# Order of the VectorE's copies, a second PSUM bank for the first projection, and the slots of the queries' transposes in a fused attention and MLP kernel

## The chip, the core and the metric

The kernel runs on one core of a Trainium2 chip. The metric is the device time of one launch in microseconds. Five engines run their own instruction streams and meet through semaphores: PE (TensorE, with its weight loads shown as PEld), DVE (VectorE), ACT (ScalarE), POOL (GpSimd) and SP (SyncE, which here only issues transfers). Matmul results go to PSUM, which this kernel holds as one tile `ps` of eight banks of 512 float32 columns and divides by hand.

## The reference

For each of 8 x 8 heads of 576 tokens and 64 dimensions: scores, a threshold at the row's maximum less `tau`, softmax over what is left, and the product with the values. The 4608 rows of 512 go through an MLP with a hard swish.

```python
def _attn_ref(q, k, v, tau):
    scores = scale * np.matmul(q, k.transpose(0, 1, 3, 2))
    thresh = np.max(scores, axis=-1, keepdims=True) - tau
    scores = np.where(scores >= thresh, scores, -1000000000.0)
    scores = scores - np.max(scores, axis=-1, keepdims=True)
    attn = np.exp(scores)
    attn = attn / (np.sum(attn, axis=-1, keepdims=True) + 1e-09)
    return np.matmul(attn, v).astype(np.float32)

def _moe_ref(x, w_in, w_out):          # x: 4608 x 512, w_in: 512 x 2048
    h = x @ w_in
    g = h * np.clip(h + 3.0, 0.0, 6.0) / 6.0
    return (g @ w_out).astype(np.float32)
```

## The kernel before, in words

**Slots.** Four heads make a quad, two a pair; there are 16 quads, and two quads are one batch element. A quad is worked in 9 slots: slots 0 to 3 take 128 queries each of the quad's first pair, 4 to 7 of its second pair, slot 8 the 64 left-over queries of both pairs. `n` counts the slots through the kernel, from 0 to 143; "slot 63" below is `n = 63`. The loop over `n` writes every engine's instructions out in order, and each engine runs them in that order; there is no scheduler behind it. A quad that is odd begins at an odd `n`.

**What a slot holds**, in the order of the loop: the two exponentials of the slot before (`sm_exp`, L309, ACT); the row maxima, which also move the scores from PSUM to SBUF (`sm_max`, L296, DVE, two instructions of 128x576) and the bias of the threshold (L299, POOL); one item of the MLP's first projection (`mm1`, L372, PE, eight matmuls for two blocks of 128 features by 256 tokens), its rectifier (`mm1_relu`: L380 on ACT in even slots, L382 on DVE in odd ones) and the product (`mm1_gate`, L387, DVE), called the gate here; the reciprocals of the slot before (`sm_recip`, L312, DVE); in even slots two quarters of a token tile of the second projection (`mm2_part`, L397, PE) and, after a tile's last quarter, its copy (`mm2_out`, L405, DVE); the masks (`sm_mask`, L304, ACT); the jobs that `plan[n]` names; the scores of coming slots (`scores`, L269, or L275 for slot 8; PE); and the normalization of the slot before (`sm_norm`, L317, POOL), which comes behind this slot's biases on POOL and needs L312.

**Jobs.** `av0`, `av0late` and `av1` multiply a pair's attention by its values (`av_main`, L341 and L344 on PE, then a copy to `xT`, L352, DVE); `avr` does the same for the left-over queries (copy L362). `q0` and `q1` transpose the queries of the next quad's first pair and of this quad's second pair. For the first two batch elements they do it on PE (L217) with a copy on DVE (L224), for the others in one DVE instruction (L226). `k0` and `k1` transpose keys on PE, with a copy on ACT (L207) from slot 22 on; `rest` does both for the left-over rows (L238, L240; copies L246 and L207).

**From slot 22 (`N1`) on** the scores of two slots are written together at the end of each odd slot: those of the odd slot in PSUM columns of banks 0, 1, 3 and 4 ("lower"), those of the even one in banks 1, 2, 4 and 5 ("upper"). Banks 2 and 5 also serve the jobs in turn (`bank()`), so a job of an odd slot must have been copied out before the last score matmuls of that slot are written. The first projection has bank 6 (`HB`), the second bank 7 (`OB`), where a token tile accumulates over two even slots.

**The projections' order.** From slot 22 each batch element has 16 items in `todo1`, one to a slot; 18 slots later the next follow. The eighth and the sixteenth item put eight quarters of the second projection into `todo2`, of which two go in each even slot. So bank 7 is in use from slot 30 to 36 and from 38 to 44, and again 18 slots later.

Of the kernel before, what the change touches and what calls it, by code (L numbers as in the profile page):

```python
# [21 lines left out]
def kernel(  # L22
# [20 lines left out]
    N1 = 22  # L43
    HB = 6
    OB = 7
# [74 lines left out]
    def load_v(b):  # L120
        vm = v_pool.tile([P, H, 4 * D], BF16, tag="vm", name="vm")
        vr = vrs[b % 2]
        vsb[b] = (vm, vr)
        for g in range(2):
            vcasts.append(lambda g=g: nc.gpsimd.dma_start(
                out=vm[:, g * 4:g * 4 + 4, :],
                in_=v[b, g * 4:g * 4 + 4, 0:512, :].rearrange("h (p t) d -> p h (t d)", t=4)))
        for a in range(2):
            vcasts.append(lambda a=a: nc.gpsimd.dma_start(
                out=vr[a * 64:(a + 1) * 64, a, :, :],  # L130
                in_=v[b, :, 512:S, :].rearrange("(hp a) p d -> a p hp d", a=2)[a]))
# [78 lines left out]
    def by_pe(pair):  # L210
        return pair // NPAIR < NB
# [77 lines left out]
    def sm_max(sl):  # L289
        sl.s = s_pool.tile([P, 2, S], F32, tag="s", name="s")  # L290
        sl.m = stat_pool.tile([P, 2], F32, tag="m", name="m")
        sl.bias = stat_pool.tile([P, 2], F32, tag="bias", name="bias")
        sl.rsum = stat_pool.tile([P, 2], F32, tag="rsum", name="rsum")
        sl.rinv = stat_pool.tile([P, 2], F32, tag="rinv", name="rinv")
        for i in range(2):
            nc.vector.tensor_scalar(out=sl.s[:, i, :], in0=score_tile(sl.n, i),  # L296
                                    scalar1=1.0, scalar2=None, op0=Alu.mult, op1=Alu.max,
                                    accum_out=sl.m[:, i:i + 1])
            nc.gpsimd.tensor_scalar(out=sl.bias[:, i:i + 1], in0=sl.m[:, i:i + 1], scalar1=-scale, scalar2=tau,  # L299
                                    op0=Alu.mult, op1=Alu.add)  # L300
# [6 lines left out]
    def sm_exp(sl, i):  # L307
        s = sl.s[:, i, :]
        nc.scalar.activation(out=s, in_=s, func=Act.Exp, accum_out=sl.rsum[:, i:i + 1])  # L309

    def sm_recip(sl):
        nc.vector.reciprocal(out=sl.rinv[:], in_=sl.rsum[:])  # L312
# [15 lines left out]
    def pe_transpose(sl):  # L328
        pb = ps_flat[:, 3072:3072 + S].bitcast(BF16).rearrange("p (c t) -> p c t", t=P)
        pn = sl.pn[:].rearrange("p a b -> p (a b)")  # L330
        for c in range(9):
            nc.tensor.transpose(pb[:, c, :], pn[:, c * P:(c + 1) * P], identb[:])
        return lambda: nc.vector.tensor_copy(out=sl.dst, in_=pb)
# [33 lines left out]
    def mm1(item, hb=HB):  # L367
        src, ni, c0, _ = item
        hps = ps[:, hb, :].rearrange("p (n w) -> p n w", n=2)
        for n in range(2):  # L370
            for ki in range(KI):
                nc.tensor.matmul(hps[:, n, :], w_in_sb[:, ki, (ni + n) * P:(ni + n + 1) * P],  # L372
                                 src[:, ki, c0:c0 + 256], start=(ki == 0), stop=(ki == KI - 1))
        return hps


    def mm1_relu(hps, on_act):
        r = r_pool.tile([P, 2, 256], F32, tag="r", name="r")[:]
        if on_act:
            nc.scalar.activation(out=r, in_=hps, func=Act.Relu, bias=three[:])  # L380
        else:
            nc.vector.tensor_scalar(out=r, in0=hps, scalar1=3.0, scalar2=0.0, op0=Alu.add, op1=Alu.max)  # L382
        return r

    def mm1_gate(item, hps, r):
        _, ni, _, g0 = item
        nc.vector.scalar_tensor_tensor(out=gbuf[:, ni:ni + 2, g0:g0 + 256], in0=r, scalar=6.0, in1=hps,  # L387
                                       op0=Alu.min, op1=Alu.mult)
# [24 lines left out]
    todo2 = []  # L413
# [16 lines left out]
    def moe_of_rest(b):  # L430
        items = [((xR[b // 4], ni, 0, M), ()) for ni in range(0, NI, 2)]
        items[-1] = (items[-1][0], [(c, 4, part) for c in (b, b - 2) for part in range(4)])
        return items
# [19 lines left out]
    plan = []  # L453
    for sl in queue:
        quad, slot = sl.quad, sl.slot
        if sl.n < N1:
            jobs = {1 if quad else 2: ["q1"], 2 if quad else 3: ["k1"], 5: ["alloc", "q0"], 6: ["k0"], 7: ["rest"],
                    8: ["av0"]}
            if quad == 0:
                jobs[1] = ["rest0"]  # L460
            else:
                jobs[3], jobs[4] = (["av1"], ["avr"]) if quad == 1 else (["av1", "avr"], [])
        elif quad % 2:
            jobs = {0: ["q1", "av0late"], 1: ["k1"], 4: ["av1", "avr"], 5: ["alloc", "k0"], 6: ["q0"], 7: ["rest"],
                    8: ["av0"]}
        else:
            jobs = {1: ["q1"], 2: ["k1"], 3: ["av1", "avr"], 4: ["alloc", "k0"], 5: ["q0"], 6: ["rest"]}
        if quad + 1 == NQUAD:
            jobs = {s: [j for j in jobs[s] if j not in ("alloc", "k0", "q0", "rest")] for s in jobs}
        plan.append(jobs.get(slot, []))  # L470

    prev = None
    for n, sl in enumerate(queue):
        quad, slot = sl.quad, sl.slot
        b, g = divmod(quad, 2)
        now = n
        if slot in (0, 4):
            pts[2 * quad + slot // 4] = pt_pool.tile([P, 9, 512], BF16, tag="pT", name="pT")
        if slot == 8:
            ptr[quad] = ptr_pool.tile([P, 9, P], BF16, tag="pR", name="pR")  # L480
        if quad == 0 and slot == 0:
            load_quad(1)
        if slot == (4 if quad else 8) and quad + 2 < NQUAD:
            load_quad(quad + 2)
        if slot == 0 and g == 1 and b + 1 < B:
            load_v(b + 1)
        if prev is not None:
            for i in range(2):
                sm_exp(prev, i)
        sm_max(sl)  # L490

        if todo1 or todo3:
            item, then = (todo1 or todo3).pop(0)
            h = mm1(item)
            r = mm1_relu(h, on_act=n % 2 == 0)
            mm1_gate(item, h, r)
            todo2.extend(then)
        copies = pe_transpose(queue[n - 2]) if n > 1 and queue[n - 2].on_chip else None
        if prev is not None:
            sm_recip(prev)  # L500
        if copies:
            copies()
        outs = []


        for _ in range(0 if n % 2 else 2):
            if todo2:
                b2, t2, part = todo2.pop(0)
                mm2_part(b2, t2, part)
                if part == 3:  # L510
                    outs += mm2_out(b2, t2, on_act=False)
        for i in range(2):
            sm_mask(sl, i)
        nxt = 2 * quad + 2
        for job in plan[n]:
            if job == "alloc":
                alloc_qk(quad + 1)
            elif job == "q1":
                transpose_q(2 * quad + 1)()
            elif job == "k1":  # L520
                transpose_k(2 * quad + 1)()
            elif job == "q0":
                transpose_q(nxt)()
            elif job == "k0":
                transpose_k(nxt)()
            elif job == "rest":
                transpose_rest(quad + 1)()
            elif job == "rest0":
                transpose_rest(0, of_k=False)()
            elif job == "av1":  # L530
                av_main(2 * quad - 1)
            elif job == "av0":
                av_main(2 * quad)
            elif job == "av0late":
                av_main(2 * quad - 2)
            elif job == "avr":
                av_rest(quad - 1)
                if quad % 2 == 0:
                    todo1.extend(moe_of(quad // 2 - 1))
                if quad % 8 == 0:  # L540
                    todo3.extend(moe_of_rest(quad // 2 - 1))
        if n == 0:
            warm_up(8)
        if n + 1 < N1:
            scores(n + 1)
        elif n % 2 and n + 2 < len(queue):
            scores(n + 1, n + 2)
        if n < 8:
            warm_up(6)
        if prev is not None:  # L550
            sm_norm(prev)
        flush()
        late.extend(outs)
        start(loads, 1)
        if n < 4 or n > 12:
            start(vcasts, 1)
        if n > 3:
            start(casts, 1 if n < 24 else 2)
        prev = sl
# [80 lines left out]
```

## Time and profile before

| | |
|---|---|
| median of 6 runs | 581.22 us (580.37 to 583.05) |
| the profiled execution | 581.61 us, of which 579.8 us from its first to its last instruction |
| PE busy | 535.4 us (92%) |
| ACT busy | 473.5 us (82%) |
| DVE busy | 424.3 us (73%) |
| POOL busy | 305.4 us (53%) |
| mean granted TensorE clock | 0.997 |

In the profile's rows a time is from the start of the span. `L372` is line 372 of the kernel before. A row of a timeline gives start, length, engine, line, operation, what is written and read, the count of merged instructions and, in brackets, the engine's idle time just before and what ended it. A merged PE row ends later than its last matmul matters: the start of the next PE row is the better mark. The slots repeat closely: the stretch of 18 slots from slot 36 to 53 takes 128.38 to 191.73 us, that from 54 to 71 191.73 to 255.07 us.

### The profile page before, as it was taken

To read this page: it belongs to the slowest core of one execution; us is meant where nothing else is said; L and a number is where in the kernel's file an instruction comes from. 1 tells how busy PE (TensorE), PEld (TensorE's weight loads), DVE (VectorE), ACT (ScalarE), POOL (GpSimd) and SP (SyncE) were. 2 spreads that over 40 slices of the span, in tenths; PEclk is the share of its full clock that TensorE was granted. 3 is DMA by queue.
4 is the path that set the end of the run, shared out by engine and by line. 5 is a ranking of instruction groups with operands and counts; after the bars stand their busy time and mean duration, and the time that the engine had idled before them with its cause. 6 is when DMAs were issued, how large, how long until landed. Compare 5 with 4: busy or idle time off the path is not lost.

```text
span 579.8 us, 12005 instructions
## 1 busy us (share of the span) xinstructions
PE 535.4 (92%) x3998; PEld 328.1 (57%) x3998; DVE 424.3 (73%) x1060; ACT 473.5 (82%) x1012; POOL 305.4 (53%) x646
## 2 busy tenths in 40 slices
PE   8898787899989998999989998999989998989997
PEld 6654454555555565555555665556555665545853
DVE  3788776687878788787878888788868888741731
ACT  4898987898988898999989898888889898851730
POOL 2789867755565555655565556555565455530000
PEclk9999998999999999999999999999999999999999
DMA  5999989986797779997897789995997744552012
GB/s 118 136 137 161 195 131 193 179 155 135 144 164 143 133 154 153 144 166 117 163 160 151 131 137 162 128 162 113 160 152 144 143 101 98 84 116 72 3 36 73
DMA packets 286350, 77.54 MB, mean 134 GB/s; under 512 B 269264, under 2 KB 281808, under 8 KB 286288
## 3 DMA queue, kind: packets, MB, share of 16 engines
q1 hardware_dynamic: 267680, 67.47, 64.2%
q0 software_dynamic: 17408, 8.92, 13.4%
q8 instruction: 31, 0.51, 0.4%
q10 hardware_dynamic: 1200, 0.39, 0.3%
q14 instruction: 31, 0.25, 0.1%
HBM read 36.70 MB, written 9.44 MB: 80 GB/s over the span
## 4 chain that ended last, share of the span: by engine, by line
PE 48%; ACT 15%; DVE 13%; issue 7%; POOL 3%; DMA 2%; SPq 0%; DVEq 0%; POOLq 0%
PE ps L397 14%; PE ps L372 14%; PE ps L269 13%; DVE s L296 7%; ACT s L304 6%; ACT s L309 5%; PE ps L341 4%; ACT r L380 4%; POOL pn L317 2%; DVE g L387 2%; PE ps L275 1%; DVE r L382 1%; DVE xT L352 1%; PE ps L344 1%; DMA pR<-pn 1%
## 5 line engine op out<-in xcount | busy, mean ns | idle before, releaser
L317 POOL TENSOR_SCALAR pn<-s,rinv 128x576 bf16<-128x576 f32 x288 | 211.7, 745 | 117.2 <-DVE rinv L312 57.0
L296 DVE TENSOR_SCALAR_CACHE_REDUCE s<-ps 128x576 f32<-128x576 f32 x288 | 206.1, 752 | 58.8 <-PE ps L269 43.4
L304 ACT ACTIVATE s<-s,bias 128x576 f32<-128x576 f32 x288 | 206.4, 765 | 23.3 <-POOL bias L299 22.7
L309 ACT ACTIVATE s<-s 128x576 f32<-128x576 f32 x288 | 192.7, 671 | 0.3
L269 PE MATMUL ps<-kT,qT 64*128 64x192 f32 (+1 forms) x1024 | 170.4, 424 | 11.7 <-DVE s L296 5.1
L372 PEld LDWEIGHTS <-w_in_sb 128*128 128x128 bf16 x1152 | 107.7, 98 | 69.2 <-issue 53.9
L372 PE MATMUL ps<-xT,w_in_sb 128*128 128x256 bf16 x1024 | 131.0, 273 | 15.9 <-DVE g L387 15.2
L397 PE MATMUL ps<-w_out_sb,g 128*128 128x512 bf16 x576 | 133.2, 379 | 0.7 <-ACT osb L403 0.7
L269 PEld LDWEIGHTS ps<-kT,qT 64*128 64x128 f32 x1024 | 95.8, 186 | 58.1 <-DVE s L296 24.6
L387 DVE SCALAR_TENSOR_TENSOR g<-r,ps 128x512 bf16<-128x512 f32 x144 | 98.9, 688 | 37.3 <-ACT r L380 35.2
L299 POOL TENSOR_SCALAR bias<-m 128x1 f32<-128x1 f32 x288 | 54.4, 189 | 90.8 <-DVE s L296 73.3
L397 PEld LDWEIGHTS <-g 128*128 128x128 bf16 x576 | 56.0, 98 | 59.5 <-issue 3.0
L380 ACT ACTIVATE r<-ps,three 128x512 f32<-128x512 f32 x86 | 58.7, 685 | 35.9 <-PE ps L372 35.3
L309 ACT ACTIVATION_READ_ACCUMULATOR s<-s 128x1 f32 x288 | 54.3, 189 | 0.0
L405 DVE TENSOR_SCALAR osb<-ps 128x512 f32<-128x512 f32 x30 | 20.7, 689 | 30.9 <-PE ps L397 30.9
L382 DVE TENSOR_SCALAR r<-ps 128x512 f32<-128x512 f32 x58 | 39.8, 687 | 0.8 <-PE ps L372 0.6
L341 PE MATMUL ps<-pT,vm 128*64 128x512 bf16 x256 | 34.5, 392 | 1.9 <-DMA pT<-pn 1.9
L312 DVE RECIPROCAL rinv<-rsum 128x2 f32<-128x2 f32 x144 | 22.9, 159 | 10.4 <-ACT s L309 10.2
L341 PEld LDWEIGHTS <-vm 128*64 128x64 bf16 x512 | 19.0, 111 | 18.9 <-issue 9.4
L207 ACT COPY kT<-ps 64x128 f32<-64x128 f32 (+1 forms) x55 | 22.8, 414 | 5.7 <-PE ps L217 2.8
L403 ACT ACTIVATE osb<-ps 128x512 f32<-128x512 f32 x5 | 3.0, 597 | 29.4 <-PE ps L397 23.2
L275 PE MATMUL ps<-kT,qT 64*64 64x384 f32 (+1 forms) x256 | 23.4, 417 | 3.3 <-DVE s L296 1.3
(43 smaller groups left out, 277.9 us busy)
## 6 DMA issues: line engine op xcount, KB each, us to landing
km<-in_k_dram SPq DMA_DIRECT2D x64, 128.0 KB, 3.0
out_dram<-osb SPq DMA_DIRECT2D x31, 256.0 KB, 2.6
nq<-in_q_dram SPq DMA_DIRECT2D x96, 72.0 KB, 2.8
vm<-in_v_dram POOLq DMA_DIRECT2D x16, 256.0 KB, 5.6
w_in_sb<-in_moe_w_in_dram POOLq DMA_DIRECT2D x16, 128.0 KB, 4.3
w_out_sb<-in_moe_w_out_dram POOLq DMA_DIRECT2D x16, 128.0 KB, 4.5
pT<-pn SPq DMA_TRANSPOSE x119, 3.5
nq<-in_q_dram SPq DMA_DIRECT2D x14, 128.0 KB, 4.7
```

What stands on the lines that cost most here:

```text
L269: nc.tensor.matmul(score_tile(n, a, k0=k0, w=w), qT_of(pair)[a * 64:(a + 1) * 64, t * P:(t + 1) * P], keys(pair, a, k0, w), start=True, st ...
L296: nc.vector.tensor_scalar(out=sl.s[:, i, :], in0=score_tile(sl.n, i), scalar1=1.0, scalar2=None, op0=Alu.mult, op1=Alu.max, accum_out=sl.m ...
L299: nc.gpsimd.tensor_scalar(out=sl.bias[:, i:i + 1], in0=sl.m[:, i:i + 1], scalar1=-scale, scalar2=tau, op0=Alu.mult, op1=Alu.add)
L304: nc.scalar.activation(out=s, in_=s, func=Act.Prelu, bias=sl.bias[:, i:i + 1], scale=scale, alpha=REJECT)
L309: nc.scalar.activation(out=s, in_=s, func=Act.Exp, accum_out=sl.rsum[:, i:i + 1])
L317: nc.gpsimd.tensor_scalar(out=pn[:, i, :], in0=sl.s[:, i, :], scalar1=sl.rinv[:, i:i + 1], scalar2=1.0, op0=Alu.mult, op1=Alu.mult)
L341: nc.tensor.matmul(pb[a * 64:(a + 1) * 64, :], vm[:, 2 * hp + a, c * D:(c + 1) * D], pT[:, 5 * a + c, cols], start=(c == 0), stop=False)
L372: nc.tensor.matmul(hps[:, n, :], w_in_sb[:, ki, (ni + n) * P:(ni + n + 1) * P], src[:, ki, c0:c0 + 256], start=(ki == 0), stop=(ki == KI - 1))
L380: nc.scalar.activation(out=r, in_=hps, func=Act.Relu, bias=three[:])
L382: nc.vector.tensor_scalar(out=r, in0=hps, scalar1=3.0, scalar2=0.0, op0=Alu.add, op1=Alu.max)
L387: nc.vector.scalar_tensor_tensor(out=gbuf[:, ni:ni + 2, g0:g0 + 256], in0=r, scalar=6.0, in1=hps, op0=Alu.min, op1=Alu.mult)
L397: nc.tensor.matmul(o_ps[0], gbuf[:, ni, g0:g0 + P], w_out_sb[:, ni, :], start=(ni == 0), stop=(ni == NI - 1))
```

## The change

It does five things. (1) In a slot whose plan has an attention product, the gate is held back until the product's copies have been given to DVE; in all other slots it stays where it was. (2) In odd slots with `todo2` empty, the first projection is written to bank 7 in place of bank 6. (3) In odd quads `av0late` stands ahead of `q1`. (4) For the first two batch elements `q0` goes from slot 23 to 24 and `q1` from slot 27 to 28. (5) The scores of slot 23 are written at the end of slot 22, on their own, and no longer with those of slot 22. The eight quarters that an item sets free enter `todo2` at the end of the slot; as such items fall in odd slots, and quarters are taken in even ones, their order stays.

```diff
         elif quad % 2:
-            jobs = {0: ["q1", "av0late"], 1: ["k1"], 4: ["av1", "avr"], 5: ["alloc", "k0"], 6: ["q0"], 7: ["rest"],
+            jobs = {0: ["av0late", "q1"], 1: ["k1"], 4: ["av1", "avr"], 5: ["alloc", "k0"], 6: ["q0"], 7: ["rest"],
                     8: ["av0"]}
+            if by_pe(2 * quad):
+                jobs[0], jobs[1] = ["av0late"], ["q1", "k1"]
         else:
             jobs = {1: ["q1"], 2: ["k1"], 3: ["av1", "avr"], 4: ["alloc", "k0"], 5: ["q0"], 6: ["rest"]}
+            if by_pe(2 * quad + 2):
+                jobs[5], jobs[6] = [], ["q0", "rest"]
...
+        gate = None
         if todo1 or todo3:
             item, then = (todo1 or todo3).pop(0)
-            h = mm1(item)
+            h = mm1(item, hb=HB if n % 2 == 0 or todo2 else OB)
             r = mm1_relu(h, on_act=n % 2 == 0)
-            mm1_gate(item, h, r)
-            todo2.extend(then)
+            gate = lambda item=item, h=h, r=r: mm1_gate(item, h, r)
+            if not any(job[:2] == "av" for job in plan[n]):
+                gate()
+                gate = None
+            late2 = then
+        else:
+            late2 = ()
...
         for job in plan[n]:
+            if gate and job[:2] != "av":
+                gate()
+                gate = None
...
+        if gate:
+            gate()
+        todo2.extend(late2)
         if n == 0:
             warm_up(8)
-        if n + 1 < N1:
+        if n <= N1:
             scores(n + 1)
         elif n % 2 and n + 2 < len(queue):
             scores(n + 1, n + 2)
```

## The prediction

> **What bounds the kernel now.** The page came first: PE is busy 92% of the span, yet the chain that ended last gives PE only 48% and the rest to ACT, DVE and POOL, so no single engine carries the time.
>
> ```profile
> PE 535.4 (92%) x3998; PEld 328.1 (57%) x3998; DVE 424.3 (73%) x1060; ACT 473.5 (82%) x1012; POOL 305.4 (53%) x646
> PE 48%; ACT 15%; DVE 13%; issue 7%; POOL 3%; DMA 2%; SPq 0%; DVEq 0%; POOLq 0%
> ```
>
> Next the waits of PE. The largest is the one that bank 7 aims at: the first projection (L372) waits until the gate (L387) of the slot before has read bank 6.
>
> ```profile
> PE ps L372 <- DVE g L387: 15.2, 16, 2.3
> PE ps L269 <- DVE s L296: 5.1, 9, 0.9
> PE ps L269 <- DVE xT L352: 1.8, 6, 0.3
> ```
>
> Then I went through the timeline slot by slot. Of the 15.2 us, 5.5 lie between slots 22 and 31 (in slots 23, 24, 27, 29 and 31: 0.21, 0.42, 2.34, 0.88 and 1.66). The others come again every 18 slots, 1.06 in slots 47, 65, 83, 101, 119 and 137 and, but for the last time, 0.58 to 1.00 two slots later. The other slots show no such wait: most of the 63.3 us of each 18 slots is PE without a gap. This is the place that repeats, slots 63 to 65:
>
> ```profile
> 221.00 0.67 DVE L405 TENSOR_SCALAR osb<-ps 128x512 f32<-128x512 f32 x1
> 221.06 1.03 PE L372 MATMUL ps<-xT,w_in_sb 128*128 128x256 bf16 x8
> ...
> 222.03 1.05 PE L341 MATMUL ps<-pT,vm 128*64 128x512 bf16 x8
> ...
> 223.22 2.20 PE L269 MATMUL ps<-kT,qT 64*128 64x192 f32 x14
> 223.66 0.69 DVE L387 SCALAR_TENSOR_TENSOR g<-r,ps 128x512 bf16<-128x512 f32 x1
> ...
> 224.34 0.76 DVE L226 STREAM_TRANSPOSE qT<-nq 128x576 f32<-128x576 f32 x1
> ...
> 225.02 0.65 DVE L352 CAST xT<-ps 128x512 bf16<-128x512 f32 x1
> ...
> 225.73 0.91 PE L269 MATMUL ps<-kT,qT 64*128 64x384 f32 x2 [0.30 <-DVE xT L352]
> ...
> 226.57 1.05 PE L372 MATMUL ps<-xT,w_in_sb 128*128 128x256 bf16 x8
> ...
> 228.38 0.69 DVE L387 SCALAR_TENSOR_TENSOR g<-r,ps 128x512 bf16<-128x512 f32 x1 [0.93 <-ACT r L380]
> ...
> 229.12 1.03 PE L372 MATMUL ps<-xT,w_in_sb 128*128 128x256 bf16 x8 [1.06 <-DVE g L387]
> ```
>
> The attention product is done on PE by 223.3, but its copy (L352) stands behind the gate and L226 and starts at 225.02. The last score matmul needs the copied bank and starts at 225.73; L372 of slot 64 follows at 226.57, then its rectifier, its gate at 228.38, and only then, with no idle in between, the maxima of slot 65 (229.06).
>
> **The first stretch, slots 22 to 31.** The gate of slot 26 ends at 92.38 and holds L372 of slot 27 to 92.44; transfers that POOL issues (0.6 to 1.1 us a slot, the last weights) stand between its normalizations and biases here.
>
> ```profile
> 92.44 1.44 PE L372 MATMUL ps<-xT,w_in_sb 128*128 128x256 bf16 x8 [2.34 <-DVE g L387]
> ...
> 105.00 0.46 POOL L299 TENSOR_SCALAR bias<-m 128x1 f32<-128x1 f32 x2
> ...
> 108.60 0.69 DVE L387 SCALAR_TENSOR_TENSOR g<-r,ps 128x512 bf16<-128x512 f32 x1 [2.36 <-ACT r L380]
> ```
>
> Walked through with the rows' durations: slot 22's scores alone take half of the 2.2 us of both, so its maxima start 1.1 earlier (74.9). But the other half now stands on PE behind `k0`, and L372 of slot 23 stays at 78.3: (5) alone gains nothing. Without `q0` in slot 23 the scores no longer wait for L224 and end some 0.85 earlier (81.75). In slot 24 DVE gets that copy (0.67) behind the gate and gives 0.6 back: the maxima of slot 25 are only 0.2 earlier. POOL has kept about 0.8 of the lead through its order, and the gate of slot 26 comes 0.8 earlier. Now bank 7: L372 of slot 27 starts at about 89.9 and not 92.44, the product ends at 92.2, its copy at 94.45 (maxima, rectifier and L312 stand before it), the scores at about 95.4 in place of 98.8. That is 3.4 us for PE, not for the end: the biases of slot 27 wait on POOL for the normalization before them and 1.1 us of issues, which puts the exponentials at 96.1, slot 28's rectifier behind them at 97.5 (99.90 before), its gate at 98.2 (100.62). From there POOL (L317, issues, L299 at 102.6 for 105.00), mask, exponential, rectifier and gate of slot 30 (106.3 for 108.60) carry **2.3 us**. `q1` in slot 28 costs DVE 0.67 before slot 29's maxima (99.6 for 101.30), which that POOL time covers. Were it not covered, 1.7 would be left.
>
> [...] The windows show the granted clock falling in this stretch:
>
> ```profile
> 92.00:94.00 2.00, 1.56 (x10) 1.33 (x10) 1.89 (x7) 2.00 (x5) 1.28 (x2) 0.73 1.27 231
> 94.00:96.00 2.00, 2.00 (x12) 0.92 (x12) 1.95 (x4) 0.79 (x3) 1.74 (x6) 0.50 1.31 254
> ```
>
> (The 0.73 and 0.50 are the clock.) [...] the rows of slot 27 take 1.44, 1.06 and 1.86 where their like take 1.03, 0.60 and 1.05, so 1.7 us more, 4.0 here. By the trace the POOL order ends last, and nothing is added. I take the trace's 2.3.
>
> **Slots 45, 63, 81, 99, 117, 135.** In slot 63 `todo2` is empty, so L372 goes to bank 7, which L405 of slot 62 reads until 221.67: it starts at 221.72, 0.66 later than now. This wait is new; behind it stand the product and the scores. The product ends at 223.96; DVE is through with maxima, rectifier (its input is there at 222.77, DVE is free at 222.94) and L312, and copies from 224.0 to 224.67. The scores take 2.14 from 223.9 (slot 67 shows 238.50 to 240.64 for the same sixteen rows), so they end at 226.04, and their last needs nothing after 224.67: **0.53 earlier** than 226.57. DVE does the gate and L226 after that; the maxima of slot 64 start at 225.9 (225.60 before) and end within 0.1 of now. That is hidden, because L372 of slot 64 and ACT's rectifier come 0.53 sooner and their gate waits for ACT (0.93 idle). So gate 64, and with no idle maxima 65, come 0.5 earlier. L372 of slot 65 loses its 1.06, but the scores at the end of slot 65 wait for maxima 65 and keep 0.5, and slot 66's rectifier waits for POOL (L317, an issue of 0.79, L299 at 231.69), which hangs on gate 64: again 0.5. Through slot 67, and then through PE's full slots, 0.5 remains: 6 x 0.52 = **3.1 us**.
>
> [...] By it every wait of L372 that bank 7 reaches returns: 0.21 + 0.42 + 2.34 + 0.88 + 6 x 1.06 = 10.2 us. The trace says that bank 7 is not free in two of the slots, and that after slot 65 POOL and ACT end last. I take the smaller.
>
> **Slots 37, 55, 73, 91, 109, 127.** Bank 7 was in use in the slot before here as well:
>
> ```profile
> 257.49 1.04 PE L372 MATMUL ps<-xT,w_in_sb 128*128 128x256 bf16 x8
> ...
> 257.69 0.69 DVE L405 TENSOR_SCALAR osb<-ps 128x512 f32<-128x512 f32 x1 [0.24 <-PE ps L397]
> ...
> 259.11 2.88 PE L269 MATMUL ps<-kT,qT 64*128 64x192 f32 x16 [0.58 <-DVE s L296]
> ```
>
> L372 starts at 258.43, 0.94 later, and ends near 259.47. Its cover is the 0.58 that PE waits for the maxima anyway, and 0.4 of the second half's wait (PEld 0.38, until 259.78). I charge 0.05 each, **0.3 us**; without cover 0.94 each, 5.6.
>
> **Held gates elsewhere** (slots 31, 35, 49, 53, 67, 71, ..., and 93, 111, 129): copies come up to 0.6 sooner, but the scores there show at most 0.2 of waiting for them on PEld and none on PE, and the held gate (until about 239.9 in slot 67) is still before the next L372 (240.64): 0, between -0.2 and +0.2 each. L312 comes earlier, but L317 stands behind the biases on POOL. No transfer is moved in any queue; nothing of SP's or POOL's order is. The quarters' later entry costs 0: they are taken in even slots only.
>
> **Sum**: -2.3 - 3.1 + 0.3 = -5.1 us. Against the profiled execution 581.61 gives 576.5; it stood 0.4 over the median of 581.22, so I say **576.2 us**.
>
> **Rivals.** *Only one part lasts* (chance 0.20): POOL in the first stretch, or the late start of slot 63, takes more than I read. One of the two gains and the 0.3 remain: 578.4 (the repeating part lost: 581.2 - 2.3 + 0.3 = 579.2; the first lost: 578.4). For it speaks that six small gains rest on margins of 0.17 (rectifier 63); against, that the slots repeat to 0.01 us. *PE is the bound* (0.04): the 10.2 us return: about 571. PE's 92% speaks for it, the chain's 48% against. *Nothing that counts* (0.07): a wait that I did not see, such as a pair of banks falling the other way, absorbs the shift: 580.5 to 582. *Slower by the new wait* (0.09): L372 behind L405 in bank 7 lands on the path. In slot 63's kind the 0.66 adds up whole, if the product, not its copy, ends last: 6 x 0.66 = 4.0; in slot 55's kind what the wait for the maxima doesn't cover, 6 x (0.94 - 0.58) = 2.2. With the first stretch's 2.3 off, 585.1. It decides from the point where L372 of slot 63 starts after 222.25 (226.57 less the 4.32 from its start to the scores' end); I have 221.72.
>
> **How the numbers follow.** My own case has 0.60 and holds 574.0 (slots 27 to 31 give 3.4, and each repeat 0.6) to 578.4. A measurement of this kernel tells about 0.3% (1.7 us) from no change, so faster means below 579.5: all of mine, the 0.04, and nearly all of the 0.20 make 0.82; same 0.09; slower 0.09. The range from 573.9 to 579.9 leaves out the slower case, the 0.04 and most of the case of nothing.
>
> **What would show it.** In the changed profile: PE L372 <- DVE g falls to about 5 us; a new PE L372 <- DVE osb L405 stands at 0.6 to 0.9 in 12 slots; PE L269 <- DVE xT is gone; the clock stays near 1.00 where it was 0.50; slots 22 to 31 take 2.3 less, each stretch of 18 slots 0.5 less. Wrong: if the stretch of 18 slots stays at 63.3 us, or L269 of slot 65 waits for something else than the maxima.

## The result and the profile after

The changed kernel takes 578.16 us (median of 15 runs, 576.54 to 581.23), the kernel before 581.43 (34 runs): ratio 0.9944, interval (95%) 0.9932 to 0.9957. It is faster by 3.3 us, where 5.0 were forecast. The profiled execution took 577.04 us, with a span of 575.3; before it was 581.61 and 579.8.

The page of the profile after, busy time by engine and the chain that ended last:

```profile
PE 531.7 (92%) x3998; PEld 326.9 (57%) x3998; DVE 425.0 (74%) x1060; ACT 473.9 (82%) x1012; POOL 305.4 (53%) x646
PE 51%; ACT 17%; DVE 10%; issue 5%; POOL 3%; DMA 1%; SPq 0%; POOLq 0%; DVEq 0%
```

The engines have the same instructions to run as before. PE's busy time is 3.7 us shorter all the same, in 18 slots of the repeat by 0.8, and there it is the score matmuls (L269, 21.0 us before, 20.0 after, for the same 128 at the same clock of 1.00): by these sums, part of what counted as busy was waiting. The waits of PE that are shown as such, after (us in total, times, longest):

```profile
PE ps L372 <- DVE osb L405: 9.4, 12, 0.8
PE ps L269 <- DVE s L296: 9.2, 12, 1.5
PE ps L372 <- DVE g L387: 4.4, 6, 1.1
```

The wait for the gate fell from 15.2 to 4.4 us, the wait of the scores for `xT` is gone, and the new wait behind the copy out of bank 7 stands in twelve slots with 0.78 each. The wait of the scores for the maxima grew from 5.1 to 9.2 us. On the two rows of L372 alone bank 7 looks like a gain of 10.8 paid with 9.4; what it is worth shows only without it.

Slots 63 to 65 after, from the timeline (start, length, and in brackets the idle time before and what ended it):

```profile
219.66 0.67 DVE L405 TENSOR_SCALAR osb<-ps 128x512 f32<-128x512 f32 x1
220.38 1.03 PE L372 MATMUL ps<-xT,w_in_sb 128*128 128x256 bf16 x8 [0.78 <-DVE osb L405]
...
222.66 0.69 DVE L352 CAST xT<-ps 128x512 bf16<-128x512 f32 x1 [0.30 <-PE ps L344]
...
224.69 1.05 PE L372 MATMUL ps<-xT,w_in_sb 128*128 128x256 bf16 x8
...
226.50 0.69 DVE L387 SCALAR_TENSOR_TENSOR g<-r,ps 128x512 bf16<-128x512 f32 x1 [0.17 <-ACT r L380]
...
227.98 2.88 PE L269 MATMUL ps<-kT,qT 64*128 64x192 f32 x16 [0.74 <-DVE s L296]
```

From L372 of slot 63 to L372 of slot 64 it is now 4.31 us (224.69 less 220.38), where it was 5.51. The start, measured from the slot's maxima, is 0.66 later. L372 of slot 65 waits no longer, but the scores of slot 65 wait 0.74 for their maxima: a stall that moved, as the prediction had it.

The windows of the repeating stretches, slots 36 to 53 and 54 to 71 (us; busy time of PE, PEld, DVE, ACT, POOL; clock; DMA share; GB/s), which were 63.35 and 63.34 us long:

```profile
127.58:190.38 62.80, 59.22 (x452) 35.87 (x451) 50.53 (x128) 57.03 (x125) 35.95 (x76) 1.00 0.83 152
190.38:253.19 62.81, 59.23 (x452) 35.90 (x451) 50.54 (x129) 57.03 (x125) 35.95 (x76) 1.00 0.88 149
```

Slot by slot against before (a slot starts with its first row maximum, L296), the whole 0.54 falls in two slots: slot 64 starts 0.62 later than the lead carried into slot 63, slot 65 then 1.16 earlier. The first stretch, slots 22 to 31, is less orderly: the start of slot 28 is 1.78 us earlier than before, that of slot 31 only 0.81, and ahead of it all, in slot 19, 1.6 us were lost in code that is the same in both kernels. The clock there was at half for 3.41 us:

```profile
66.07:69.48 3.41, 3.41 (x17) 2.24 (x17) 2.13 (x5) 3.21 (x8) 2.77 (x6) 0.50 0.90 161
```

### The profile page after: what moved, and what is told of

Read it like the earlier page. It is cut to its first block, busy times and chain, and to the rows that moved or that the text cites. A ratio compares the mean times of both kernels' runs of the same rounds, so it can differ in the third digit from the quotient of the medians.

```text
span 575.3 us, 11988 instructions
## 1 busy us (share of the span) xinstructions
PE 531.7 (92%) x3998; PEld 326.9 (57%) x3998; DVE 425.0 (74%) x1060; ACT 473.9 (82%) x1012; POOL 305.4 (53%) x646
## 4 chain that ended last, share of the span: by engine, by line
PE 51%; ACT 17%; DVE 10%; issue 5%; POOL 3%; DMA 1%; SPq 0%; POOLq 0%; DVEq 0%
PE ps L372 15%; PE ps L269 14%; PE ps L397 14%; ACT s L304 7%; DVE s L296 6%; ACT s L309 6%; PE ps L341 5%; ACT r L380 4%; POOL pn L317 2%; PE ps L275 1%; DVE g L387 1%; DVE osb L405 1%; PE ps L344 1%; ACT kT L207 1%; DVE r L382 1%
## 5 line engine op out<-in xcount | busy, mean ns | idle before, releaser
L317 POOL TENSOR_SCALAR pn<-s,rinv 128x576 bf16<-128x576 f32 x288 | 211.7, 745 | 107.0 <-DVE rinv L312 52.0
L296 DVE TENSOR_SCALAR_CACHE_REDUCE s<-ps 128x576 f32<-128x576 f32 x288 | 205.8, 752 | 52.5 <-PE ps L269 38.3
L269 PE MATMUL ps<-kT,qT 64*128 64x192 f32 (+1 forms) x1024 | 166.9, 425 | 13.8 <-DVE s L296 9.2
L372 PEld LDWEIGHTS <-w_in_sb 128*128 128x128 bf16 x1152 | 107.6, 98 | 66.8 <-issue 52.3
L372 PE MATMUL ps<-xT,w_in_sb 128*128 128x256 bf16 x1024 | 130.5, 273 | 13.8 <-DVE osb L405 9.4
L269 PEld LDWEIGHTS ps<-kT,qT 64*128 64x128 f32 x1024 | 95.2, 187 | 56.7 <-DVE s L296 24.1
L299 POOL TENSOR_SCALAR bias<-m 128x1 f32<-128x1 f32 x288 | 54.4, 189 | 97.0 <-DVE s L296 79.1
L405 DVE TENSOR_SCALAR osb<-ps 128x512 f32<-128x512 f32 x30 | 20.6, 688 | 30.9 <-PE ps L397 30.9
L275 PE MATMUL ps<-kT,qT 64*64 64x384 f32 (+1 forms) x256 | 23.4, 417 | 3.3 <-DVE s L296 1.3
```

Of the source, the lines that this page charges most:

```text
L269: nc.tensor.matmul(score_tile(n, a, k0=k0, w=w), qT_of(pair)[a * 64:(a + 1) * 64, t * P:(t + 1) * P], keys(pair, a, k0, w), start=True, st ...
L317: nc.gpsimd.tensor_scalar(out=pn[:, i, :], in0=sl.s[:, i, :], scalar1=sl.rinv[:, i:i + 1], scalar2=1.0, op0=Alu.mult, op1=Alu.mult)
```

## The experiments

Three theories were held against each other: that, as in the prediction, bank 7 frees the projection and the held gate brings the copy forward; that the copy's place ahead of the queries' transpose does the work, and bank 7 only adds its wait; and that much of the difference in the first stretch comes from the clock and not from the order of the work.

**Bank 7 taken out.** Everything else as after:

```diff
-            h = mm1(item, hb=HB if n % 2 == 0 or todo2 else OB)
+            h = mm1(item)
```

> The changed kernel with every first projection in bank 6 again; all else is kept. Theory (the product's copy ahead of the gate makes the gain of slots 63 to 68, the wait behind L405 is mostly covered but takes half of what that order could give): the wait of 0.78 in slot 63 is gone, the scores of slot 63 end about 0.5 earlier than in the changed kernel, and each stretch of 18 slots takes 0.3 to 0.5 us less than the changed kernel's 62.8; the first stretch loses the start of slot 27 and slots 22 to 31 take 0.5 to 1.5 us more. Sum -2 to -1 us against the changed kernel, about 576.5. Rival (bank 7 makes the gain, by taking away the wait of L372 for the gate in slots 47, 65 and so on): each stretch of 18 slots is back at 63.3, the sum at 581.

572.98 us, ratio 0.9839 (0.9819 to 0.9859): 5.2 us faster than the change as it was made. The expectation had the sign right and the size too small (1 to 2 us). The same slots in its timeline:

```profile
218.07 0.68 DVE L405 TENSOR_SCALAR osb<-ps 128x512 f32<-128x512 f32 x1
218.13 1.03 PE L372 MATMUL ps<-xT,w_in_sb 128*128 128x256 bf16 x8
...
220.69 0.67 DVE L352 CAST xT<-ps 128x512 bf16<-128x512 f32 x1
...
222.44 1.05 PE L372 MATMUL ps<-xT,w_in_sb 128*128 128x256 bf16 x8
...
224.25 0.69 DVE L387 SCALAR_TENSOR_TENSOR g<-r,ps 128x512 bf16<-128x512 f32 x1 [0.17 <-ACT r L380]
...
224.99 1.03 PE L372 MATMUL ps<-xT,w_in_sb 128*128 128x256 bf16 x8 [0.88 <-DVE g L387]
```

L372 of slot 63 starts beside L405, not behind it, and the next L372 again follows 4.31 us later: the shorter way is the same in both, and bank 7 only puts its wait in front. Slot 65 has its old wait back (0.88), and it costs nothing. The stretch of 18 slots:

```profile
126.65:188.79 62.14, 59.28 (x452) 35.87 (x451) 50.43 (x128) 57.02 (x125) 36.08 (x76) 1.00 0.83 152
```

So a repeat gains 1.20 us without bank 7 and 0.54 with it. Six times the difference of 0.66 are 4.0 of the 5.2 us; in the two profiles 0.93 us more lie ahead of slot 36, and their mean granted clocks are 0.996 with bank 7 and 0.999 without it.

**Bank 7 only where it is idle**, so neither in slot 63's kind nor in slot 55's, but still in slots 47, 65 and in the first stretch. `used` is the slot that last wrote a quarter of a token tile there:

```diff
+    used = -1
...
-            h = mm1(item, hb=HB if n % 2 == 0 or todo2 else OB)
+            h = mm1(item, hb=HB if n % 2 == 0 or todo2 or n - 1 == used else OB)
...
                 mm2_part(b2, t2, part)
+                used = n
```

> The changed kernel, with the first projection in bank 7 only if the slot before wrote no token tile there: slots 37, 45, 55, 63, 73 and so on are back in bank 6. Theory: the 12 waits behind L405 (9.4 us in sum) vanish, the six in slots 45, 63, ... give 0.3 to 0.5 us each and those in slots 37, 55, ... nothing; the first stretch keeps its bank 7: 2 to 3 us less than the changed kernel, about 575.5. Rival (those waits are hidden whole, since the second half of the maxima of slot 64 ends last): no change, 578.

573.45 us, ratio 0.984 (0.9818 to 0.9862), and 62.15 us for the 18 slots: the same as with no bank 7 at all. The harm is the wait behind L405, 0.66 us in each of slots 45, 63, 81, 99, 117 and 135, and in the repeats it helps nothing where the bank is free.

**The swap alone**, in the kernel before:

```diff
-            jobs = {0: ["q1", "av0late"], 1: ["k1"], ...
+            jobs = {0: ["av0late", "q1"], 1: ["k1"], ...
```

> The kernel before, with av0late ahead of q1 as the only edit: no held gate, no bank 7, queries where they were, scores of slots 22 and 23 together. Theory (L226 ahead of the copy is most of what the scores of slot 63 wait for): the copy moves from 225.02 to about 224.35, the scores end 0.6 earlier, each stretch of 18 slots takes 62.7 to 62.9 and the sum is 3 us under the kernel before. Rival (the gate ahead of the copy matters as much, or bank 7 is needed too): less than 0.2 per stretch, the sum within 1 us of the kernel before.

577.74 us, ratio 0.9921 (0.9897 to 0.9945); 62.68 us for the 18 slots, 0.66 less than before, as expected. One word moved equals the whole change in time, within the noise.

**The held gate alone**, with `q1` still first and bank 6:

```diff
-            mm1_gate(item, h, r)
-            todo2.extend(then)
+            gate = lambda item=item, h=h, r=r: mm1_gate(item, h, r)
+            if not any(job[:2] == "av" for job in plan[n]):
+                gate()
+                gate = None
...
```

> The kernel before with the held gate as the only edit: av0late still stands behind q1, so in slot 63 the gate still goes ahead of L226 and the copy; only slots with av1, avr or av0 as first job change. Theory (the held gate is worth 0.5 in slot 63 only with av0late first, and nothing in the other slots): each stretch of 18 slots 63.3 us, the sum within 0.5 of the kernel before. Rival (earlier copies in slots 67, 71 and so on give something too): 0.1 to 0.4 less for each stretch, 1 to 3 us.

580.82 us, ratio 0.9989 (0.9975 to 1.0003), no difference that the runs can tell, and 0.07 less in each repeat of the profile. The reason stands in the loop over the jobs: the held gate is released before the first job that is not a product, and with `q1` first that is at once. The product's copy comes after the gate and L226:

```profile
223.89 0.77 DVE L226 STREAM_TRANSPOSE qT<-nq 128x576 f32<-128x576 f32 x1
...
224.59 0.65 DVE L352 CAST xT<-ps 128x512 bf16<-128x512 f32 x1
```

**Swap and held gate together**, in the kernel before, without bank 7, the queries' slots and the single scores:

```diff
-            jobs = {0: ["q1", "av0late"], 1: ["k1"], ...
+            jobs = {0: ["av0late", "q1"], 1: ["k1"], ...
...
-            mm1_gate(item, h, r)
+            gate = lambda item=item, h=h, r=r: mm1_gate(item, h, r)
...
```

> The kernel before with two of the five edits: the held gate and av0late ahead of q1; bank 6 alone, queries in slots 23 and 27, scores of slots 22 and 23 together. Theory (these two carry the change, the swap 0.66 and the held gate another 0.54 for each repeat; queries' slots and single scores are worth under 0.7 in the first stretch): 62.1 us for each stretch of 18 slots, median 573.5 to 574.5, within 1 us of the experiment without bank 7. Rival (queries' slots and single scores carry 1 us or more): 575 or over.

573.89 us, ratio 0.9857 (0.9833 to 0.9881):

```profile
128.41:190.54 62.13, 58.80 (x445) 35.83 (x451) 50.41 (x129) 57.02 (x125) 36.03 (x76) 1.00 0.86 157
```

The 1.20 of a repeat is complete with these two: 0.66 by the swap, 0.54 more by the held gate, which needs the swap.

**The first stretch: scores of slots 22 and 23 together again, or the queries back in odd slots.** The first takes (5) out of the change, the second (4):

```diff
-        if n <= N1:
+        if n + 1 < N1:
             scores(n + 1)
```

> The changed kernel with the scores of slots 22 and 23 written together again at the end of slot 21. Theory: slot 22 begins 1.05 later, slot 23 no later, since the scores of slot 23 no longer stand behind the keys' transposes in slot 22; the end of slot 31 stays within 0.5 us and the sum within 0.5 of the changed kernel. Rival (the single scores are what leads the first stretch): 1 to 2 us more than the changed kernel.

```diff
-            if by_pe(2 * quad):
-                jobs[0], jobs[1] = ["av0late"], ["q1", "k1"]
...
-            if by_pe(2 * quad + 2):
-                jobs[5], jobs[6] = [], ["q0", "rest"]
```

> The changed kernel with the queries' transposes back in slots 23 and 27 (behind av0late there); bank 7, held gates and single scores are kept. Theory (in the first stretch the copies of the queries cost DVE in slots 24 and 28 what they save PE in slots 23 and 27): slots 24 and 28 take 0.7 to 0.9 us less, slots 23 and 27 0.4 to 1.5 more, and from slot 20 to slot 31 it is within 0.5 us of the changed kernel; stretches after slot 36 are the same to 0.05. Rival (the move carries the first stretch's gain): 1 to 2 us more there. The sum within 1 us of the changed kernel by the theory; single sums can differ by the place of a half-clock stretch of 3.4 us.

579.85 us (20 runs; ratio 0.9965, 0.995 to 0.9981) and 578.64 (20 runs; 0.9937, 0.9918 to 0.9955). The single scores are worth 1.7 us beside the rest of the change by the medians, 1.2 by the ratios, so the rival came closer than the theory; but it need not all be their order: the profile without them has a mean granted clock of 0.991, that of the change 0.996. The queries' place, 0.5 us by the medians and nothing by the ratios, cannot be told from nothing in these times. The profile of the second shows more, up to the start of slot 31. From slot 20 to there the change takes 2.30 us less than the kernel before, with the queries back it takes 1.53 less. By the author's estimate, which takes the clock as full in both (the change's was 1.00 from 84 to 114 us), their place gives 0.77, between the theory's 0.5 and the rival. In slot 31 the left-over queries' attention landed late, PE stood 3.18 us, and the sixteen score matmuls behind it took 4.21 us, where their like in slot 63 of the change take 2.21.

```profile
113.94 0.43 PE L341 MATMUL ps<-pR,vm 128*64 128x64 bf16 x8 [3.18 <-DMA pR<-pn]
...
114.61 4.21 PE L269 MATMUL ps<-kT,qT 64*128 64x192 f32 x16
```

**Four more filler transposes a slot, up to slot 21**, to keep PE busy; added to the kernel without bank 7:

```diff
         if n < 8:
             warm_up(6)
+        elif n < N1:
+            warm_up(4)
```

> The kernel without bank 7 with four more idle transposes on PE at the end of each slot from 8 to 21 (some 0.4 us each, in PE's gaps; they compute nothing that is used). Theory [...]: half-clock stretches before slot 22 are gone or rarer, but PE's work in slots with few gaps adds 0 to 2 us; the median lies between -1 and +2 us of the one without bank 7, with less spread. Rival (the half-clock stretches do not follow PE's gaps): as many, 1 to 3 us slower.

573.63 us (572.41 to 580.8), ratio 0.9874 (0.9827 to 0.992): no gain over 572.98, and more spread and not less. Its profile had a wait of 4.3 us for `pR` in slot 31, outside the slots that were filled, and a mean granted clock of 0.996, where that of the version without the filler was 0.999. On the clock this is inconclusive.

**Fewer transfers issued ahead of POOL's biases.** The prediction says that POOL's order (L317, an issue, L299) ends last after slot 65. Two versions on top of the one without bank 7 issue the values' conversions only in a quad's slots 5 to 8, the first from slot 36 on, the second from slot 13 on:

```diff
-        if n < 4 or n > 12:
+        if n < 4 or 12 < n < 36 or (n > 35 and slot > 4):
             start(vcasts, 1)
```

> The changed kernel with bank 6 alone (as in the experiment without bank 7) and, from slot 36 on, the four transfers of the next values issued by POOL in slots 5 to 8 of the odd quads and no longer in slots 0 to 3 (before slot 36 they are where they were). Theory (from the gate of slot 64 to that of slot 66 POOL's normalization, its issue of 0.8 us and the bias behind it end last): the biases of slot 65 and 67 come 0.6 to 0.8 earlier, the rectifier of slot 66 too, and each stretch of 18 slots that loads values takes 0.4 to 1.0 us less than the 62.1 without bank 7: five of them, 2 to 5 us, about 569.5. Rival (the scores of slots 66 and 67 on PE, or ACT's own work, end last there): no change, 573.

```diff
-        if n < 4 or n > 12:
+        if n < 4 or (n > 12 and slot > 4):
             start(vcasts, 1)
```

> The changed kernel without bank 7 and with the values' transfers issued in slots 5 to 8 of the odd quads throughout, so also behind slot 31. Theory (in slots 27 to 31 POOL's order ends last as in slots 64 to 67, and the last weights come earlier once the values' issues are out of their way): slots 27 to 31 take 0.5 to 1 us less than in the experiment that left them there, no wait for w_out in slot 32 and none for pR in slot 31; median 569 to 570. Rival (the values' transfers, moved under slots 32 to 35, meet the output and the keys there): 0 to 1 us slower than 570.8.

570.77 us (ratio 0.98, 0.9769 to 0.9831) and 569.09 (568.72 to 569.42; ratio 0.9773, 0.9747 to 0.9798). Against the one without bank 7 the first gains 2.2 us, the low end of what was expected, the second 3.9, as expected. POOL in slot 65 (the normalization of slot 63, an issue, the biases of slot 65), first the kernel without bank 7, then the second version:

```profile
225.27 1.48 POOL L317 TENSOR_SCALAR pn<-s,rinv 128x576 bf16<-128x576 f32 x2 [0.91 <-DVE rinv L312]
226.68 0.79 POOL L125 DMA_DIRECT2D vm<-in_v_dram  x1
227.56 0.46 POOL L299 TENSOR_SCALAR bias<-m 128x1 f32<-128x1 f32 x2
```

```profile
224.37 1.47 POOL L317 TENSOR_SCALAR pn<-s,rinv 128x576 bf16<-128x576 f32 x2 [0.91 <-DMA nq<-in_q_dram]
225.93 0.47 POOL L299 TENSOR_SCALAR bias<-m 128x1 f32<-128x1 f32 x2
```

From L317 to the biases it is 1.56 us and no longer 2.29, and slot 67 starts 0.53 earlier for it. It is not free: in slot 57 the transfer of `pR` now lands late, which cost this stretch 0.98; the stretches from slots 36 and 72 have the 0.53 without the loss.

```profile
198.47 0.32 PE L341 MATMUL ps<-pR,vm 128*64 128x64 bf16 x8 [1.15 <-DMA pR<-pn]
```

**The same on swap and held gate alone.** The edit of the second version, on the kernel before with those two:

> The kernel before with the held gate, av0late ahead of q1, and the values' transfers in slots 5 to 8 of the odd quads throughout. Theory: as the other kernel with these transfers moved throughout, but for the first stretch: 569.5 to 571.5; [...] Rival (the queries' move and the single scores pay): 1 to 2 us more than that other kernel.

570.18 us (569.83 to 575.59), ratio 0.9812 (0.9777 to 0.9848). It lies in the expected range, but the difference of 1.1 from that other kernel is the rival's: the queries' slots and the single scores together are worth about 1 us once bank 7 is out, 1.1 here and 0.9 between 573.89 and 572.98. In the profiles of both pairs it is 0.98 from slot 19 to slot 31. The best version of all keeps (1), (3), (4) and (5), leaves (2) out and moves the values' conversions: 569.09 us (four runs), 2.3% below the kernel before.

**The change once more**, for its spread:

> The changed kernel as it is, for a second profile. Theory (half-clock stretches of 3.4 us and late landings in slots 17 to 32 move from run to run, the repeats do not): each stretch of 18 slots 62.8 to 0.02 us, as before; the slots at half clock are others than slot 19, or the end of slot 36 differs by 0.5 to 3 us from the first profile. Rival (the first stretch is as fixed as the repeats): slot 19 is at half clock again, and slot 36 starts within 0.1 us of 127.58.

578.48 us, ratio 0.9932 (0.9906 to 0.9958), and a profile whose first stretch differs from the one above: 0.90 us less than before from slot 19 to 31, with a half-clock stretch of its own, now in slot 25 (0.50 from 87.69 to 91.10 us). The theory came true.

## Why the prediction was right, and where it was wrong

**Right in direction, 2 us too far.** The measured 578.16 lies in the range, and at the edge of the prediction's own case (574.0 to 578.4). It lies nearer to its rival "only one part lasts" with the first stretch lost, 578.4, and by the parts below that is closer to what happened: the repeats held, and most of the first stretch did not. (The last step of the sum is also off by 0.1: 576.5 less 0.4 is 576.1.)

**Slots 45, 63, ...: right.** 0.52 each was forecast, 0.54 measured, six times: 3.24 us. The steps came true one by one (L372 0.66 later, product, copy directly behind it, the gate of slot 64 waiting for ACT, the stall passed on to the scores of slot 65). What the prediction did not see is that its 0.52 is a difference: 1.20 from the copy's new place, less 0.66 for the wait, so that bank 7 works against the other two edits here. The rival "slower by the new wait" priced the six waits at 4.0 us, and that is what they cost (6 x 0.66); they did not make the kernel slower than before because the other two edits paid more.

**Slots 37, 55, ...: 0.3 forecast, nothing measured.** Slot 73 and slot 74 both start 1.88 us earlier than before, though L372 of slot 73 waits 0.78. The cover named there held in full.

**The held gates elsewhere: 0 forecast, right in the slots, but with a gain at the end.** In the profiles of the change, of the held gate alone and of swap and held gate together, PE's last wait for `pT` is about half a microsecond shorter, no longer 1.9 but this:

```profile
PE ps L341 <- DMA pT<-pn: 1.3, 1, 1.3
```

From the start of slot 143 to the end the kernel takes 71.56 us where it took 72.10, 0.54 less. This was not in the sum.

**The first stretch: 2.3 forecast; this is the step that failed.** The prediction walked the stretch in the one profile that it had, saw the clock fall to 0.50 there (from 92.92 to 96.34), and wrote that by the trace POOL's order ends last and "nothing is added" by the clock. But a sum read off the rows of that execution held the clock already. The kernel with the held gate alone issues the same instructions in the same order as the kernel before up to the gate of slot 27. Here are the 3.41 us that hold its largest wait and the 3.41 us after them in the kernel before, then the same place with the held gate alone:

```profile
89.51:92.92 3.41, 1.07 (x11) 0.81 (x9) 2.42 (x7) 3.38 (x9) 2.11 (x6) 1.00 1.25 185
92.92:96.34 3.42, 3.42 (x18) 1.94 (x17) 2.92 (x8) 2.21 (x7) 3.16 (x7) 0.50 1.28 228
```

```profile
88.00:92.00 4.00, 2.44 (x27) 1.31 (x25) 1.88 (x6) 3.46 (x8) 3.49 (x9) 1.00 1.10 138
92.00:94.00 2.00, 1.23 (x12) 1.14 (x11) 1.97 (x5) 2.00 (x5) 0.94 (x2) 1.00 1.28 200
94.00:96.00 2.00, 2.00 (x21) 1.11 (x21) 2.00 (x7) 0.78 (x3) 1.84 (x5) 1.00 1.24 256
```

Both have the wait of 2.34 us ahead of L372 of slot 27, up to 92.44 in the one and 92.77 in the other. In the kernel before, PE is busy for 1.07 of the first 3.41 us, and the next 3.41 us run at a clock of 0.50. In the other, PE is busy for 2.44 of the 4.00 us from 88.00, and the clock stays at 1.00. Why it fell in the one and not in the other is not shown. Slot 27 takes 6.62 us in the one and 5.00 in the other, and from slot 19 to slot 31 the second is 1.60 us shorter; the swap alone, also at full clock there, is 1.47 shorter, swap and held gate together 1.30. So about 1.6 of the 2.3 us forecast was, by the author's estimate from these runs, the clock of one execution. The change in full has 2.30 between slots 20 and 31, which is the forecast to the digit, but luck as far as the cause goes: some 0.7 of it is left against a kernel before at full clock. Nor is bank 7 needed for it, on which the walk rests for slot 27: the version without it has 2.28 from slot 19. The order within the stretch was read correctly (slot 22 starts 1.07 earlier and gives it back before slot 23, as walked, slot 27 gains most); the term's size was not. A sign like "slots 22 to 31 take 2.3 less" could not tell the two causes apart.

Beside its 2.3 the prediction weighed the slowdown of slot 27's rows, which it put at 1.7 us; by these runs it was 1.6. But the 4.0 that it made of it counts this twice, since the 2.3 held it.

**What the sum leaves open.** Undisturbed, the parts give -3.24 - 0.7 - 0.54 = -4.5 us; the medians differ by 3.3. The author's estimate is that half-clock stretches of the change's own make the missing 1.2 us; that is not shown. In slot 25 the product in bank 7 and the missing `q0` put PE's two waits of 0.73 and 0.59 (so without bank 7) into one of 1.48, and in the repeated run the clock falls to 0.50 behind it:

```profile
86.83 2.64 PE L269 MATMUL ps<-kT,qT 64*128 64x192 f32 x8 [1.48 <-DVE s L296]
```

```profile
84.28:87.69 3.41, 1.91 (x15) 1.28 (x15) 3.23 (x9) 3.08 (x8) 2.46 (x6) 1.00 0.94 170
87.69:91.10 3.41, 3.41 (x22) 1.42 (x20) 1.03 (x3) 3.13 (x8) 2.82 (x7) 0.50 1.18 156
```

(Both fences are of the repeated run of the change.) The sixteen matmuls of L275 behind this wait take 2.01 us there, and 2.20 in the version with bank 7 only where it is idle, which has the same wait of 1.48. In the first profile of the change the wait is 1.48 too, and they take 1.20, at a clock of 1.00; they take 1.20 as well in the version without bank 7 and in the best version, where the waits are two shorter ones (0.73 and 0.59, 0.72 and 0.59). The mean granted clock of the profile of before, which has one stretch of 3.41 us at 0.50, is 0.997. The mean clock was at or below 0.997 in 14 of 15 runs of the change, and in 40 of the 79 runs of the kernel before that have it on record. Those 40 took 582.9 us in the mean, the other 39 581.2; the one run of the change above 0.997 is its fastest, 576.54, and 4.7 us under those 39. That is a correlation; no run here changed the clock by itself, and the one that tried to (the filler transposes) settled nothing.

**The 10.2 us.** The waits of L372 that bank 7 reaches add up to 10.2 us, and the prediction weighed that all of them return. Bank 7 returned nothing where it was free (573.45 us with it there, 572.98 without it) and cost 4.0 us where L405 was still reading it (six times 0.66).

## What to carry to other kernels

Price each edit of a bundle apart, against the bundle without it and not against the kernel before: here the forecast came true for the repeats while one edit ate more than half of what two others gained. In this kernel the second bank was free only when its last reader was done (in the profile of the change L372 waited 0.78 us for L405 in each of twelve slots); look for who reads it, in the slot before, before you count the wait that it removes. And when the profile of before shows a low clock in the very place of the change, work the sum for both clocks: one execution's slow stretch is not the kernel's (slot 27 ran at 0.50 before and at 1.00 with the held gate alone).

## What the hardware showed that was not expected

In these profiles PE's busy time alone does not tell the half clock. The stretches at 0.50 that the fences above show in the profiles of before, of the change and of its repeat, from 92.92, 66.07 and 87.69 us, each lasted 3.41 us. In the 3.41 us ahead of them PE was busy for 1.07, 2.21 and 1.91 us. The best version kept full clock after 3.41 us in which PE was busy for 1.70, less than two of these.

```profile
90.12:93.53 3.41, 1.70 (x16) 1.11 (x17) 3.01 (x9) 3.37 (x8) 2.45 (x7) 1.00 1.29 140
```

What decides it stays open. The 3.41 us at half clock went with 1.6 us lost in slot 27 before and 1.6 us in slot 19 of the change. That the runs of the change spread over 4.7 us, where the four of the best version lie within 0.7, may come from such stretches (an estimate, not shown), and from transfers that land late in one run and not in the next: PE waited 3.18 and 4.3 us for `pR` in two of the profiles, and 1.7 us for output weights in that of the swap alone.
